# A transformer block on one core: normalised rows and k masks on VectorE, batched powers, paced v projections, blank matmuls in idle units

## The chip, the cores and the metric

The kernel runs on one core of a Trainium2 chip. The core has five engines that run side by side, each with its own queue of instructions taken in order: TensorE (PE in the profile; its weight loads are PEld) for matmuls, ScalarE (ACT) for table functions such as exp, VectorE (DVE) and GpSimd (POOL) for elementwise work, and SyncE (SP), which here issues all DMAs. Engines wait for each other through semaphores. Matmul results go to PSUM, eight banks of 128 x 512 fp32, which POOL does not read in this kernel; everything else lies in SBUF. The metric is the device time of one execution, in microseconds (us).

## What is computed

A layer norm, then attention and a gated feed-forward layer on the same normalised rows, both added to the input. In short:

```
xn  = (x - mean) / sqrt(var + 1e-5)                  # x: 2048 x 512, bf16
qkv = xn @ wqkv                                      # 32 heads of 16
p   = softmax(q @ k.T / 4)                           # per head, 2048 x 2048
att = (p @ v, heads side by side) @ wo
h   = max(xn @ W_gate, 0) * (xn @ W_up)              # 2048 x 1792
out = x + att + h @ W_down
```

The softmax is 32 x 2048 x 2048 exponentials. The kernel leaves out the subtraction of the maximum, and takes the sums from a column of ones beside v.

## The kernel before

The sequence is cut into 16 tiles of 128 rows (m or kt) and four blocks of 512 (b for keys, c4 for queries). The heads are cut into four groups gg of eight; in a group, ee picks the even or the odd heads and j one of four row strips of 32 partitions. kT holds each k projection twice, once with the odd and once with the even heads set to zero (the mask hmask), so that a score matmul can work on a strip of 32 rows.

The attention runs through tiles (c4, gg, ee, kt, j) in that order; three tiles make a **unit**, and there are 683 units. A unit is: up to three score matmuls into one of two score slots of three PSUM banks (L760), one exponential over 128 x 1536 from there into a slot of a ring of 13 (L772), and, as soon as all four strips of a kt are there, four matmuls of p with v (L736) into PSUM bank 0 of ps_b. Scores of unit u need the exponential of unit u-2 to be done, for the slot. When a (c4, gg, ee) is complete, `normalise` copies the sums out (L707), inverts them by way of two small DMAs, and POOL multiplies (L722).

Everything else is put between the units. `ln_block` makes the normalised and transposed rows xnT of a block: statistics on VectorE (L450, L451), variance plus eps and a power of -1/2 on POOL (L452, L454), the normalised row on POOL (L461), four transposes on TensorE (L478) and an eviction (L484 on ScalarE for block 0, L492 on VectorE for the others). x_sb has room for two blocks, so the loads of blocks 2 and 3 (L407) wait until the rows of blocks 0 and 1 are normalised. `proj_q`, `proj_k` and `proj_v` are chains of four matmuls (`mm_chain`, L510), nearly all into bank 1 of ps_b, with an eviction each; `proj_k` copies the bank to kp on VectorE (L539), and POOL makes the two masked halves from it (L542). Only the very first k projection is masked from PSUM by VectorE (L535). `glu` makes the hidden layer (L608, L612) and `out_rows` the output rows.

The order of each engine's queue is worked out on the host by a planner (`Graph.run`): every operation has an assumed duration and latency, a priority (lower goes first), and perhaps a unit `after` which it comes; the planner plays the program through by these numbers, and what it starts first on an engine stands first in that engine's queue. On the chip the order is fixed, and only the waits are real. The assumed durations are the second arguments of `G.op`: 450 ns for a normalised row and for a k mask on POOL, for example. Jobs (projections, hidden layer, output rows) are assigned to units in a list `plan`, at most one job step to a unit; a step is two matmuls of a chain. By the calls of `job` the steps are 24 for k, 30 for q, 224 for the hidden layer and 176 for output rows. The first group's k and all v projections stand outside this plan, with negative priorities.

At the start TensorE runs 14 matmuls on zeros (L567), and the first score may start when block 0 is normalised and its q and k are projected.

## Time and profile before

| | us |
|---|---|
| three runs of before | 1002.39, 1002.51, 1010.9; median 1002.51 |
| profiled execution, its own time | 1008.92 |
| its span, first to last instruction | 1007.0 |
| ScalarE busy in it | 929.3 |
| TensorE busy | 779.0 |
| VectorE busy | 173.1 |
| POOL busy | 138.5 |
| mean granted clock of TensorE | 0.848 |

The profile is one execution on the chip. Its page gives busy times, 40 slices of the span (the row PEclk is the clock granted to TensorE in tenths), the chain of work that ended last, and groups of instructions; the trace behind it answers for any stretch. A group row reads: line, engine, operation, what it writes and reads, shapes, count, then busy us and mean ns of one, then the idle time of the engine before them and what ended it. A timeline row reads: start and length in us, engine, line, operation, tiles, shapes, and how many instructions in a row it merges, with the idle time before the first in square brackets. A row of windows gives a stretch, its length, and for each engine the busy time and the count. Ends of matmuls are modelled, so a busy TensorE need not be one at its peak.

### The profile page before, as it was taken

How to read it: one execution, taken by the hardware profiler on the slowest of the kernel's cores; microseconds unless marked ns; L12 is line 12 of the kernel's file. 1: busy time of each engine (PE TensorE's matmuls, PEld its weight loads, DVE VectorE, ACT ScalarE, POOL GpSimd, SP SyncE). 2: the span in 40 equal slices, each digit the busy share in tenths (PEclk: the TensorE clock that was granted, in tenths of full speed). 3: DMA queues.
4: the chain of work that ended last, by engine and by line, in shares of the span. 5: the costliest groups of instructions: out<-in, count | busy, mean ns of one | idle time of the engine just before them, and what ended most of it. 6: DMA issues, size and time to landing. Idle time of an engine off the chain costs nothing.

```text
span 1007.0 us, 11864 instructions
## 1 busy us (share of the span) xinstructions
PE 779.0 (77%) x5078; PEld 184.7 (18%) x5166; DVE 173.1 (17%) x292; ACT 929.3 (92%) x690; POOL 138.5 (14%) x120
## 2 busy tenths in 40 slices
PE   4659877787778878877778888777777888888882
PEld 2212111111112211111111221111111221222220
DVE  3423212121100111211100002111110002321021
ACT  2449999999999999999999999999999999999992
POOL 8861504122000000000000000000000000000000
PEclk7679889887859987898867998888785999999995
DMA  4300200111000011111000012101100012221000
GB/s 125 116 1 25 62 17 17 32 32 33 12 22 22 18 37 43 43 43 35 10 11 27 27 38 48 38 16 33 43 12 22 26 34 54 53 54 27 22 12 33
DMA packets 84084, 34.59 MB, mean 34 GB/s; under 512 B 69952, under 2 KB 79936, under 8 KB 84032
## 3 DMA queue, kind: packets, MB, share of 16 engines
q1 hardware_dynamic: 84032, 33.83, 12.8%
q8 instruction: 41, 0.67, 0.3%
q14 instruction: 11, 0.09, 0.0%
HBM read 31.20 MB, written 2.36 MB: 33 GB/s over the span
## 4 chain that ended last, share of the span: by engine, by line
ACT 78%; PE 14%; POOL 5%; issue 1%; another core or an unknown queue 1%; DVE 1%; DMA 0%; ACTq 0%; SPq 0%
ACT ring L772 78%; PE ps_b L510 6%; PE ps_sc L760 5%; POOL xn_sb L461 3%; PE ps_b L736 3%; POOL rstd L454 1%; POOL kT L542 1%; POOL vare L452 0%; DMA x_sb<-in_A_x_dram 0%; DVE xn_sb L648 0%; DMA rsum<-o_sb 0%; DVE kp L539 0%; PE ps_sc L510 0%; PE ps_b L478 0%
## 5 line engine op out<-in xcount | busy, mean ns | idle before, releaser
L772 ACT ACTIVATE ring<-ps_sc 128x1536 bf16<-128x1536 f32 (+1 forms) x683 | 925.0, 1647 | 43.8 <-PE ps_sc L760 41.6
L760 PE MATMUL ps_sc<-qT,kT 32*128 32x512 bf16 x2048 | 300.9, 435 | 171.0 <-ACT ring L772 138.8
L736 PE MATMUL ps_b<-ring,v_aug 128*17 128x512 bf16 x2048 | 224.7, 432 | 5.0 <-DVE o_sb L707 2.0
L760 PEld LDWEIGHTS ps_sc<-qT,kT 32*128 32x128 bf16 x2048 | 67.6, 93 | 440.3 <-ACT ring L772 376.3
L722 POOL TENSOR_TENSOR x_sb<-o_sb,rb 128x512 bf16<-128x512 f32 x20 | 25.4, 1269 | 556.6 <-DMA rb<-rec_scr 556.6
L736 PEld LDWEIGHTS ps_b<-ring,v_aug 128*17 128x17 bf16 x2048 | 49.4, 88 | 198.8 <-issue 188.0
L510 PE MATMUL ps_b<-xnT,wus 128*128 128x512 bf16 x194 | 76.1, 469 | 5.4 <-issue 5.2
L608 DVE COPY up_sb<-ps_b 128x512 f32<-128x512 f32 x56 | 38.7, 692 | 239.7 <-PE ps_b L510 229.4
L510 PE MATMUL ps_b<-xnT,wgs 128*128 128x512 bf16 x213 | 70.8, 413 | 2.1 <-issue 1.8
L510 PE MATMUL ps_b<-Wd,hT 128*128 128x512 bf16 x206 | 66.5, 399 | 3.1 <-issue 3.1
L612 DVE SCALAR_TENSOR_TENSOR hT<-ps_b,up_sb 128x512 bf16<-128x512 f32 x56 | 38.7, 692 | 110.3 <-PE ps_b L510 107.8
L542 POOL TENSOR_SCALAR kT<-kp,hmask 128x512 bf16<-128x512 bf16 x30 | 46.6, 1566 | 65.6 <-DVE kp L539 64.1
L722 POOL TENSOR_TENSOR oT<-o_sb,rb 128x512 bf16<-128x512 f32 x12 | 15.2, 1270 | 233.5 <-DMA rb<-rec_scr 233.5
L707 DVE COPY o_sb<-ps_b 128x512 f32<-128x512 f32 x32 | 22.1, 690 | 133.4 <-PE ps_b L736 133.4
L648 DVE TENSOR_TENSOR xn_sb<-ps_b,xr_sb 128x512 bf16<-128x512 f32 x12 | 8.3, 692 | 146.8 <-PE ps_b L510 146.8
L461 POOL TENSOR_SCALAR xn_sb<-x_sb,mv,rstd 128x512 bf16<-128x512 bf16 x16 | 33.4, 2091 | 0.2
L510 PE MATMUL ps_b<-Wo_p,x_sb 128*128 128x512 bf16 x71 | 22.6, 387 | 11.8 <-POOL x_sb L722 10.9
L510 PE MATMUL ps_b<-xnT,Wk 128*128 128x512 bf16 x60 | 21.1, 444 | 1.1 <-issue 0.8
L510 PE MATMUL ps_b<-Wv,xnT 128*128 128x512 bf16 x60 | 20.7, 449 | 1.2 <-issue 0.4
L510 PEld LDWEIGHTS ps_b<-xnT,wus 128*128 128x128 bf16 x224 | 13.7, 103 | 34.0 <-issue 31.7
L510 PEld LDWEIGHTS ps_b<-xnT,wgs 128*128 128x128 bf16 x224 | 13.1, 99 | 31.3 <-issue 23.0
L510 PE MATMUL ps_b<-xnT,Wq 128*128 128x512 bf16 x52 | 17.5, 407 | 1.3 <-issue 1.3
(51 smaller groups left out, 161.8 us busy)
## 6 DMA issues: line engine op xcount, KB each, us to landing
rb<-rec_scr SPq DMA_DIRECT2D x32, 256.0 KB
wus<-in_B_W_up_dram SPq DMA_DIRECT2D x56, 128.0 KB, 2.5
wgs<-in_B_W_gate_dram SPq DMA_DIRECT2D x56, 128.0 KB, 2.3
xr_sb<-in_A_x_dram SPq DMA_DIRECT2D x16, 128.0 KB, 4.6
out_dram<-xn_sb SPq DMA_DIRECT2D x16, 128.0 KB, 1.7
Wd<-in_B_W_down_dram SPq DMA_DIRECT2D x1, 1792.0 KB, 8.0
x_sb<-in_A_x_dram SPq DMA_DIRECT2D x3, 512.0 KB, 4.0
Wv<-in_A_wqkv_dram SPq DMA_DIRECT2D x1, 512.0 KB, 7.8
```

Of the source, the lines that this page charges most:

```text
L454: G.op("POOL", 300, lambda e, m=m: e.tensor_tensor(rstd[:, m:m + 1], vare[:, m:m + 1], expo[:, 0:1], ALU.pow), reads=[t_ve, t_expo], write ...
L461: G.op("POOL", 450, lambda e, m=m, t=t_n: e.tensor_scalar(xn_sb[:, t.slot, :], xs(m), mv[:, m, 0:1], rstd[:, m:m + 1], op0=ALU.subtract, o ...
L510: ins = e.matmul(bank_of(tile, sub), l(), r(), start=(i == 0), stop=(i == n - 1))
L542: G.op("POOL", 450, lambda e, ee=ee: e.tensor_scalar(dsts[ee], kp[:, tkp.slot, :], hmask[:, ee:ee + 1], None, op0=ALU.mult), reads=[tkp, t ...
L608: G.op("DVE", 690, lambda e: e.tensor_copy(up_sb[:, tup.slot, :], bank_of(tu)), reads=[tu], writes=[tup], prio=slots[1])
L612: G.op("DVE", 690, lambda e: e.scalar_tensor_tensor(out=hT[:, FT * th.slot + ft, :], in0=bank_of(tg), scalar=0.0, in1=up_sb[:, tup.slot, : ...
L648: G.op("DVE", 690, lambda e: e.tensor_tensor(xn_sb[:, to_.slot, :], bank_of(t, sub), xr_sb[:, txr.slot, :] if first else resid(i), ALU.add ...
L707: G.op("DVE", 690, lambda e: e.tensor_copy(o_sb[:, to.slot, :], ps_b[:, 0, :]), reads=[tp], writes=[to], prio=-950, name="oev%d" % n)
L722: G.op("POOL", 1200, lambda e: e.tensor_tensor(oT_of(tn), o_sb[:, to.slot, :], rb[:, trb.slot, :], ALU.mult), reads=[to, trb], writes=[tn] ...
L736: ins = e.matmul(ps_b[32 * j:32 * j + VN, 0, :], v_aug[:, kt, 8 * gg + 2 * j + ee, 0:VN], ring[:, UNIT * tr.slot + i, :], start=(kt == 0), ...
L760: ins = e.matmul(ps_sc[:, 3 * ts.slot + i, :], kT[32 * j:32 * j + 32, 2 * gg + ee, 128 * kt:128 * kt + 128], qT[32 * j:32 * j + 32, t_q[(c ...
L772: return e.activation(ring[:, UNIT * tr.slot:UNIT * tr.slot + n, :], ps_sc[:, 3 * ts.slot:3 * ts.slot + n, :], ACTF.Exp, scale=0.25)
```

## The change

Six edits. (1) The normalised row (16 times) moves from POOL to VectorE, with 360 ns assumed. (2) For blocks 1 to 3 the variance and the power are done once for four tiles, [128, 4], after all four aggregates; block 0 keeps one per tile. (3) All k projections are masked by VectorE from PSUM, as the first one was; the buffer kp, its pool and its copy go, and the two masks follow each other. (4) The v projection of tile kt is held back in the plan until unit 1.3 kt, and keeps its negative priority then. (5) The memset of the ones beside v is no longer held until unit 2. (6) A unit beyond 24 to which no job step is assigned issues two matmuls of zeros by zeros into the first bank of its score slot, ahead of its score matmuls, which overwrite that bank; the planner's duration for the scores stays 330 ns. With the edits the planner works out new orders for all engines.

```diff
@@ -340,7 +340,6 @@
         hT = sb("hT", [128, NHT * FT, 512], BF16)
         up_sb = sb("up_sb", [128, NUP, 512], FP32)
         o_sb = sb("o_sb", [128, 2, 512], FP32)
-        kp = sb("kp", [128, 3, 512], BF16)
         rb = sb("rb", [128, 2, 512], FP32)
         rsum = sb("rsum", [128, 2, 16], FP32)
         rrec = sb("rrec", [128, 2, 16], FP32)
@@ -363,7 +362,6 @@
         P_oT = Pool("oT", 14)
         P_x = Pool("x", 2)
         P_xr = Pool("xr", 2)
-        P_kp = Pool("kp", 3)
 
 
         t_id, t_pid, t_mask, t_mask0, t_expo, t_warm, t_zero = (Tile() for _ in range(7))
@@ -384,7 +382,7 @@
                                                     base=0, pattern=[[-1, 128]], channel_multiplier=1),
              reads=[t_id], writes=[t_id], prio=-898)
         t_vones, t_woz = Tile(), Tile()
-        G.op("POOL", 2500, lambda e: e.memset(v_aug[:, :, :, DH:VN], 1.0), writes=[t_vones], prio=-500, after=2)
+        G.op("POOL", 2500, lambda e: e.memset(v_aug[:, :, :, DH:VN], 1.0), writes=[t_vones], prio=-500)
         G.op("POOL", 4200, lambda e: e.memset(Wo_p[:], 0.0), writes=[t_woz], prio=20, after=30)
 
         t_pvz = Tile("pvz", P_b, [0])
@@ -444,21 +442,31 @@
 
             first = b == 0
             t_rs = [Tile() for _ in range(4)]
+            t_mvs = Tile()
+
+            def inv(m, n, rd, wr):
+                t_ve = Tile()
+                G.op("POOL", 230, lambda e: e.tensor_scalar(vare[:, m:m + n], mv[:, m:m + n, 1], EPS, None, op0=ALU.add),
+                     reads=[rd], writes=[t_ve], prio=pr)
+                G.op("POOL", 400 + 160 * n, lambda e: e.tensor_tensor(rstd[:, m:m + n], vare[:, m:m + n], expo[:, 0:n], ALU.pow),
+                     reads=[t_ve, t_expo], writes=[wr], prio=pr)
             for i in range(4):
                 m = 4 * b + i
-                t_st, t_mv, t_ve = Tile(), Tile(), Tile()
+                t_st, t_mv = Tile(), Tile()
                 G.op("DVE", 640, lambda e, m=m: e.bn_stats(stats[:, m, :], xs(m)), reads=[t_xm[m]], writes=[t_st], prio=pr)
-                G.op("DVE", 120, lambda e, m=m: e.bn_aggr(mv[:, m, :], stats[:, m, :]), reads=[t_st], writes=[t_mv], prio=pr - 0.1)
-                G.op("POOL", 100, lambda e, m=m: e.tensor_scalar(vare[:, m:m + 1], mv[:, m, 1:2], EPS, None, op0=ALU.add),
-                     reads=[t_mv], writes=[t_ve], prio=pr)
-                G.op("POOL", 300, lambda e, m=m: e.tensor_tensor(rstd[:, m:m + 1], vare[:, m:m + 1], expo[:, 0:1], ALU.pow),
-                     reads=[t_ve, t_expo], writes=[t_rs[i]], prio=pr)
+                G.op("DVE", 130, lambda e, m=m: e.bn_aggr(mv[:, m, :], stats[:, m, :]), reads=[t_st], writes=[t_mv], prio=pr - 0.1)
+                t_mvs.w.append(G.ops[-1])
+                if first:
+                    inv(m, 1, t_mv, t_rs[i])
+            if not first:
+                inv(4 * b, 4, t_mvs, t_rs[0])
+                t_rs = [t_rs[0]] * 4
             if first:
                 tp0, tp1 = Tile("tp0", P_sc, [0]), Tile("tp1", P_sc, [1])
             for i in range(4):
                 m = 4 * b + i
                 t_n = Tile("xn", P_xn)
-                G.op("POOL", 450, lambda e, m=m, t=t_n: e.tensor_scalar(
+                G.op("DVE", 360, lambda e, m=m, t=t_n: e.tensor_scalar(
                     xn_sb[:, t.slot, :], xs(m), mv[:, m, 0:1], rstd[:, m:m + 1], op0=ALU.subtract, op1=ALU.mult),
                     reads=[t_xm[m], t_rs[i]], writes=[t_n], prio=pr + 0.2)
                 t_x[b].r.append(G.ops[-1])
@@ -510,7 +518,7 @@
                         ins = e.matmul(bank_of(tile, sub), l(), r(), start=(i == 0), stop=(i == n - 1))
                     return ins
                 G.op("PE", dur * (min(a + per, n) - a) + 100, fn, reads=reads, writes=[tile],
-                     prio=slots[k] if slots else prio, after=slots[k] if slots else None)
+                     prio=prio if prio < 0 else slots[k] if slots else prio, after=slots[k] if slots else None)
 
         def proj_q(c4, gg, prio=0.0, tile=None, sub=0, eng="DVE", slots=None):
             t = tile or Tile("pq", P_b, [1])
@@ -523,29 +531,21 @@
             else:
                 G.op("DVE", 690, lambda e: e.tensor_copy(qT[:, tq.slot, :], bank_of(t, sub)), reads=[t], writes=[tq], prio=prio)
 
-        def proj_k(gg, b, prio=0.0, tile=None, sub=0, slots=None, gap=0.5):
+        def proj_k(gg, b, prio=0.0, tile=None, sub=0, slots=None, gap=0.02):
             t = tile or Tile("pk", P_b, [0, 1] if (gg, b) in ((0, 1), (0, 2)) else [1])
             prio = slots[-1] if slots else prio
             mm_chain(t, [((lambda dt=dt: Wk[:, dt, 128 * gg:128 * gg + 128]), (lambda dt=dt: xnT[:, dt, 512 * b:512 * b + 512]))
                          for dt in range(DT)], [t_wk[gg], t_xnT[b]], prio, sub=sub, slots=slots)
             dsts = [kT[:, 2 * gg + ee, 512 * b:512 * b + 512] for ee in range(2)]
-            if (gg, b) == (0, 0):
-                for ee in range(2):
-                    tk = t_k[(gg, ee, b)] = Tile("k")
-                    G.op("DVE", 690, lambda e, ee=ee: e.tensor_scalar(dsts[ee], bank_of(t, sub), hmask[:, ee:ee + 1], None, op0=ALU.mult),
-                         reads=[t, t_masks[ee]], writes=[tk], prio=prio + 0.01 * ee)
-                return
-            tkp = Tile("kp", P_kp)
-            G.op("DVE", 690, lambda e: e.tensor_copy(kp[:, tkp.slot, :], bank_of(t, sub)), reads=[t], writes=[tkp], prio=prio)
             for ee in range(2):
                 tk = t_k[(gg, ee, b)] = Tile("k")
-                G.op("POOL", 450, lambda e, ee=ee: e.tensor_scalar(dsts[ee], kp[:, tkp.slot, :], hmask[:, ee:ee + 1], None, op0=ALU.mult),
-                     reads=[tkp, t_masks[ee]], writes=[tk], prio=prio + gap * ee)
+                G.op("DVE", 690, lambda e, ee=ee: e.tensor_scalar(dsts[ee], bank_of(t, sub), hmask[:, ee:ee + 1], None, op0=ALU.mult),
+                     reads=[t, t_masks[ee]], writes=[tk], prio=prio + gap * ee)
 
         def proj_v(kt, prio, allowed=(1,)):
             t = Tile("pv", P_b, list(allowed))
             mm_chain(t, [((lambda dt=dt: xnT[:, dt, 128 * kt:128 * kt + 128]), (lambda dt=dt: Wv[:, dt, :]))
-                         for dt in range(DT)], [t_wv, t_xnT[kt // 4]], prio)
+                         for dt in range(DT)], [t_wv, t_xnT[kt // 4]], prio, slots=[1.3 * kt] * 2)
             tv = t_v[kt] = Tile("v")
             G.op("DVE", 690, lambda e: e.tensor_copy(v_aug[:, kt, :, 0:DH], bank_of(t).rearrange("p (h d) -> p h d", h=H)),
                  reads=[t], writes=[tv], prio=prio)
@@ -571,10 +571,10 @@
         pb = Tile("pro", P_sc, [1])
         proj_q(0, 0, -790, tile=pb, sub=1, eng="ACT")
         tk_t = Tile("prok", P_b, [1])
-        proj_k(0, 0, -789, tile=tk_t, gap=8)
+        proj_k(0, 0, -789, tile=tk_t, gap=0.02)
         for b in range(1, NB):
             ln_block(b, -700 + 10 * b)
-            proj_k(0, b, -695 + 10 * b, gap=8)
+            proj_k(0, b, -695 + 10 * b, gap=0.02)
         for kt in range(NT):
             proj_v(kt, -684 + 10 * (kt // 4) + 0.1 * kt, allowed=(0, 1) if kt < 8 else (1,))
 
@@ -695,6 +695,7 @@
                 cur += 1.0
             plan.append((s[0] - lead, s, fn))
         plan.sort(key=lambda j: j[0])
+        busy = {int(p) for _, s, _ in plan for p in s}
 
 
         pv_tile, last_rec, where = {}, {}, {}
@@ -754,8 +755,12 @@
             ts = Tile("s%d" % u, P_sc)
             n = len(cl)
 
-            def sc(e, ts=ts, cl=cl):
+            def sc(e, ts=ts, cl=cl, idle=u > 24 and u not in busy):
                 ins = None
+                if idle:
+
+                    for _ in range(2):
+                        e.matmul(ps_sc[:, 3 * ts.slot, :], zeros[:, 0:128], zeros[:], start=True, stop=True)
                 for i, (c4, gg, ee, kt, j) in enumerate(cl):
                     ins = e.matmul(ps_sc[:, 3 * ts.slot + i, :], kT[32 * j:32 * j + 32, 2 * gg + ee, 128 * kt:128 * kt + 128],
                                    qT[32 * j:32 * j + 32, t_q[(c4, gg)].slot, :], start=True, stop=True, tile_position=(32 * j, 0))
```

## The prediction

> **What bounds the kernel now.** I read the page first: busy times, the granted clock over the span, and the chain that ended last.
>
> ```profile
> PE 779.0 (77%) x5078; PEld 184.7 (18%) x5166; DVE 173.1 (17%) x292; ACT 929.3 (92%) x690; POOL 138.5 (14%) x120
> PEclk7679889887859987898867998888785999999995
> ACT 78%; PE 14%; POOL 5%; issue 1%; another core or an unknown queue 1%; DVE 1%; DMA 0%; ACTq 0%; SPq 0%
> ```
>
> ScalarE, with its exponentials, is the limit; the rest of the chain is what keeps it from running. So the second view is ScalarE's timeline, whose rows end where it sat idle, and the third the same work in two windows.
>
> ```profile
> 16.68 1.08 ACT L484 ACTIVATE xnT<-ps_sc 128x512 bf16<-128x512 bf16 x2 [4.99 <-PE ps_sc L478]
> 22.80 2.79 ACT L772 ACTIVATE ring<-ps_sc 128x1536 bf16<-128x1536 f32 x2 [2.45 <-PE ps_sc L760]
> 44.59 1.45 ACT L772 ACTIVATE ring<-ps_sc 128x1536 bf16<-128x1536 f32 x1 [4.84 <-PE ps_sc L760]
> 60.90 2.79 ACT L772 ACTIVATE ring<-ps_sc 128x1536 bf16<-128x1536 f32 x2 [11.94 <-PE ps_sc L760]
> 76.29 46.24 ACT L772 ACTIVATE ring<-ps_sc 128x1536 bf16<-128x1536 f32 x34 [0.20 <-PE ps_sc L760]
> 777.11 211.97 ACT L772 ACTIVATE ring<-ps_sc 128x1536 bf16<-128x1536 f32 x158 [0.50 <-PE ps_sc L760]
> ```
>
> ```profile
> 22.80:76.29 53.49, 26.80 (x20) 0.72 0.19 55
> 76.29:989.10 912.81, 898.16 (x664) 0.87 0.12 30
> ```
>
> The last timeline row gives the undisturbed period: 158 exponentials in 211.97 us, 1.341 each. Against it the profiled execution splits into 22.8 before the first exponential; 53.5 in which 19 finish (25.5 at the period, 28.0 lost); 912.8 for the other 664 (890.4, 22.4 lost); and a tail of 17.9 from 989.1 to 1007.0. The change can win from the first 22.8, from the 28.0 and from the 22.4.
>
> **Front end.** Who kept ScalarE waiting there is read from the groups of instructions and POOL's timeline.
>
> ```profile
> L542 POOL TENSOR_SCALAR kT<-kp,hmask 128x512 bf16<-128x512 bf16 x30 | 46.6, 1566 | 65.6 <-DVE kp L539 64.1 <-DVE mv L451 1.5
> L461 POOL TENSOR_SCALAR xn_sb<-x_sb,mv,rstd 128x512 bf16<-128x512 bf16 x16 | 33.4, 2091 | 0.2
> L454 POOL TENSOR_TENSOR rstd<-vare,expo 128x1 f32<-128x1 f32 x16 | 8.8, 562 | 0.2
> L492 DVE COPY xnT<-ps_b 128x1024 bf16<-128x1024 bf16 x6 | 4.1, 690 | 11.9 <-PE ps_b L478 11.9
> L535 DVE TENSOR_SCALAR kT<-ps_b,hmask 128x512 bf16<-128x512 f32 x2 | 1.4, 746 | 8.5 <-PE ps_b L510 8.5
> L377 DVE TENSOR_SCALAR hmask<-pid 128x1 f32<-128x1 int32 x1 | 0.2, 154 | 0.0
> ```
>
> ```profile
> 5.13 1.09 POOL L454 TENSOR_TENSOR rstd<-vare,expo 128x1 f32<-128x1 f32 x2
> 6.22 4.17 POOL L461 TENSOR_SCALAR xn_sb<-x_sb,mv,rstd 128x512 bf16<-128x512 bf16 x2
> 10.37 0.41 POOL L452 TENSOR_SCALAR vare<-mv 128x1 f32<-128x1 f32 x2
> 48.37 4.17 POOL L461 TENSOR_SCALAR xn_sb<-x_sb,mv,rstd 128x512 bf16<-128x512 bf16 x2
> 58.62 3.11 POOL L542 TENSOR_SCALAR kT<-kp,hmask 128x512 bf16<-128x512 bf16 x2
> ```
>
> POOL normalises a 128-row tile in 2.09 us and masks a k half in 1.57, with no idle time before the normalised rows. The 11.94 us hole ahead of the exponential at 60.90 is the two masks of row 58.62, queued behind normalised rows of the next block (48.37 on). The orders were planned with 450 ns for either.
>
> **Its pieces after the change.** The normalised row on VectorE is not in the trace. Ends: 0.15 us (a one-column tensor_scalar, L377) and 0.75 (L535, from PSUM). Nearest is L492, bf16 to bf16: (690-154)/1024 = 0.52 ns an element, so 154 + 512 x 0.52 = 0.42 us, which I take. A k mask costs the measured 0.70 (1.41 for two); the copy to kp (0.69) goes, so VectorE gains 0.7 per projection. The batched power over four columns lies between 0.56 (one) and 2.25 (four); I take 1.1.
>
> ```profile
> 5.99 0.30 DVE L451 BATCH_NORM_AGGREGATE mv<-stats 128x2 f32<-128x6 f32 x2
> 10.07 1.29 DVE L450 BATCH_NORM_STATS2 stats<-x_sb 128x6 f32<-128x512 bf16 x2 [3.78 <-DMA x_sb<-in_A_x_dram]
> 17.82 1.89 PE L510 MATMUL ps_sc<-xnT,Wq 128*128 128x512 bf16 x4 [0.75 <-ACT xnT L484]
> 16.01 11.55 SPq L407 DMA_DIRECT2D x_sb<-in_A_x_dram  x2
> ```
>
> First exponential: statistics end at 6.3 as before. POOL's first two powers end at 6.22, and the other two (0.41 + 1.09) now follow at once, by 7.7. The rows come from VectorE at about 6.7, 7.1, 7.9 and 8.4, the last transposes end near 8.9 and ScalarE's last eviction near 9.7 instead of 17.76. From Wq's first matmul (17.82) to the first exponential it is 4.98 us, unchanged: 9.7 + 5.0 = 14.7, so 8.1 us won. VectorE is then free of block 1's statistics (10.07 to 13), so the first masks lose little.
>
> After it every block of k lasts 16/3 units, 7.15 us of exponentials. A block asks of VectorE four statistics and aggregates (3.4), four rows (1.7), two transposed copies (1.4), two masks (1.4) and four v copies (2.8): 10.7 us. Three blocks behind 10.07 would end at 42, and the third must be masked by 14.7 + 16 x 1.341 = 36.2. But the second masks (2.1 in all) may come a pass later, and so, thanks to the new pacing and the 13 slots of the ring, may some eight v copies (5.5); with block 0's masks (1.4) VectorE needs until 10.07 + 32.1 - 7.6 + 1.4 = 36. It just fits if dense. TensorE is as full there: four v matmuls take 1.7 us at half clock (17.82: 1.89 for four, starts 0.42 apart). The x loads move too: SyncE issued blocks 2 and 3 at 16.01 and about 27.2, behind POOL's rows; now near 8.5 and 17, and the weight loads queued behind them come earlier with them. For order and waits I take 8 us lost in place of 28.0, with ends 0 (it fits) and 28 (VectorE as jammed as POOL). The memset of v_aug (2.29) drops into POOL's idle time ahead of its first variance at 4.76; cover gone, it costs at most 2.3. Later k masks hold bank 1 0.7 us longer, 12 times: between 0 and 8.4; I take 0, since VectorE is busy 17% and TensorE has slack between score groups, shown next.
>
> **The blank matmuls.** Windows of all engines at single-clock stretches; the columns are busy time of PE, PEld, DVE, ACT, POOL, then granted clock.
>
> ```profile
> 6.00:8.00 2.00, 0.45 (x3) 0.00 (x0) 0.29 (x3) 0.00 (x0) 2.00 (x2) 1.00 1.05 328
> 73.70:77.10 3.40, 3.40 (x15) 0.76 (x13) 0.69 (x1) 3.20 (x3) 2.75 (x1) 0.50 0.00 0
> 77.10:118.00 40.90, 36.33 (x264) 9.43 (x267) 13.46 (x21) 40.78 (x32) 13.65 (x9) 1.00 0.15 42
> 275.10:305.80 30.70, 24.64 (x137) 4.35 (x135) 0.94 (x2) 29.98 (x23) 1.27 (x1) 0.50 0.06 18
> 305.80:367.20 61.40, 51.12 (x358) 12.64 (x362) 5.35 (x9) 61.40 (x47) 2.54 (x2) 1.00 0.10 29
> ```
>
> From 275.1 to 305.8 no projection fills the units (scores and p times v alone): the clock stays at 0.50. From 305.8 to 367.2 nearly every unit has its two projection matmuls: 1.00 throughout, and no idle ScalarE. The 22.4 us are lost where such units alternate: projection matmuls then meet the half clock and delay the scores. Two blank matmuls make an idle unit as full as a busy one. Zeros count: the clock is 1.00 at 6 to 8, behind nothing but the zero-operand warm-up. By the list of jobs 24 + 30 + 224 + 176 = 454 of 683 units are busy; some 208 of those beyond unit 24 get blanks.
>
> ```profile
> 849.68 2.81 ACT L772 ACTIVATE ring<-ps_sc 128x1536 bf16<-128x1536 f32 x2
> 849.86 0.39 PE L760 MATMUL ps_sc<-qT,kT 32*128 32x512 bf16 x3
> 850.19 0.60 PE L510 MATMUL ps_b<-xnT,wgs 128*128 128x512 bf16 x2
> 850.72 0.39 PE L736 MATMUL ps_b<-ring,v_aug 128*17 128x512 bf16 x4
> ```
>
> ```profile
> 43.94 0.61 PE L760 MATMUL ps_sc<-qT,kT 32*128 32x512 bf16 x3
> 63.70 0.39 PE L760 MATMUL ps_sc<-qT,kT 32*128 32x512 bf16 x3
> 64.14 1.45 ACT L772 ACTIVATE ring<-ps_sc 128x1536 bf16<-128x1536 f32 x1 [0.44 <-PE ps_sc L760]
> ```
>
> The blanks stand in front of the scores and behind the wait for the score bank, so they lengthen ScalarE's loop. At full clock scores start 0.18 after an exponential (849.68 to 849.86), two full matmuls take 0.53 (850.19 to 850.72), and an exponential follows its scores by 0.44 (63.70 to 64.14): 1.15, under the period of 1.341. They cost nothing, with 0.19 to spare. At half clock the matmuls take about 0.95 (two at 0.42, and 0.1 for the switch) and the scores 0.65 (43.94 to 44.59): 1.78, or 0.44 late per idle unit. But then TensorE is busy without a break, and in row 73.70 such a stretch (3.40 of 3.40) is followed by 41 us at 1.00. I take the 22.4 as won whole, with ends 0 won and, below nothing, the loss of the rival below.
>
> **Sum.** 14.7 + 683 x 1.341 (915.9) + 8 + 0 + 17.9 = 956.5 us of span. The profiled execution of before took 1008.9 for a span of 1007.0; with the same 1.9 I predict **958 us**, 5.0% under its own time and 4.4% under the median of 1002.5. The profiled execution lies 6.4 above that median, and I subtract nothing for it: what spreads the runs is probably the clock, which is wanted steady here.
>
> **Rivals.** (a) *VectorE, or TensorE under it, jams the front end*: the block-by-block waits stay at some 23 us lost instead of 8, giving 973. For it: demand fits only if dense. Against: nothing there is as slow as POOL's 2.09. (b) *The blanks leave the clock as it is*, and the 22.4 stay: 981. Against: rows 275.10 and 305.80 differ by just such matmuls. In the Trainium skill, TensorE: Matmul & The Clock Gate, section HAM oscillation, the rule is "no PE-idle gaps >~3.4µs"; by that rule the small gaps of idle units would not lower the clock, filling them would not raise it, and the time would be the 981 of this rival. The trace disagrees: 0.50 in row 275.10 with TensorE busy 24.64 of 30.70 us. (c) *Blanks late at full clock too*, by 0.15 us a unit: 208 x 0.15 = 31, giving 989. Against: 0.19 to spare; for it: the loads of the blank weights may not hide as L510's do. (d) *Slower*: blanks keep the loop at half clock, 0.44 late in every idle unit, 208 x 0.44 = 92: 1050. It decides from (1002.5 - 958)/208 = 0.21 per unit, half of the idle units at half clock. Against: row 73.70.
>
> **Numbers.** Forecast 0.58, (a) 0.20, (b) 0.08, (c) 0.11, (d) 0.03. The forecast's own range is 948 to 968 (first exponential and front-end loss off by some 10). The whole range, 946 to 980, takes in (a) and leaves out (c), (d) and most of (b). A difference under about 1% this kernel's measurement cannot tell from none; 1% under the median is 992.5, so faster 0.95 (all but (d) and late versions of (c)), within 1% 0.03, slower 0.02.
>
> **What would show it.** First exponential near 14.7; the last hole over 2 us before about 45; no POOL row of xn_sb or kT; the row on VectorE near 0.42 us. Granted clock near 1.0 in nearly all slices between the front end and the tail, and ScalarE rows at 1.341 per exponential in stretches that had idle units. Wrong would be holes of ScalarE ended by PE in idle units, or slices at half clock; or a front end in which VectorE is busy nine tenths and ScalarE waits on it.

## The result and the profile after

The changed kernel takes 971.6 us, the median of three runs (968.6 to 971.9), against 1002.5 before: 0.965 of the time, 95% interval 0.958 to 0.972. The profiled execution took 971.9 us, its span is 970.0. 958 was predicted, with 946 to 980 as the whole range: the direction and that range held, the gain was 30.9 us where 44.5 was forecast. The time lies outside the 948 to 968 that the prediction named as the forecast's own range, in the part that was kept for a jammed front end.

From the page of the changed kernel, busy times, granted clock by slices, and the chain that ended last:

```profile
PE 804.9 (83%) x5482; PEld 205.6 (21%) x5584; DVE 192.6 (20%) x323; ACT 925.9 (95%) x690; POOL 54.0 (6%) x56
PEclk8899999999999999999999999999999999999996
ACT 82%; PE 12%; DVE 3%; DMA 1%; issue 1%; SPq 0%; POOLq 0%; ACTq 0%
```

The clock row is the first thing to compare: 25 of 40 slices stood below 9 tenths before, now only the two of the front end and the tail do. POOL had 5% of the chain and has none now but its queue. ScalarE's timeline after, to be read as before (start, length, the idle time ahead in brackets):

```profile
11.39 1.08 ACT L492 ACTIVATE xnT<-ps_sc 128x512 bf16<-128x512 bf16 x2 [2.29 <-PE ps_sc L486]
17.64 13.66 ACT L777 ACTIVATE ring<-ps_sc 128x1536 bf16<-128x1536 f32 x10 [2.59 <-PE ps_sc L765]
35.54 4.14 ACT L777 ACTIVATE ring<-ps_sc 128x1536 bf16<-128x1536 f32 x3 [4.24 <-PE ps_sc L765]
42.11 1.45 ACT L777 ACTIVATE ring<-ps_sc 128x1536 bf16<-128x1536 f32 x1 [2.43 <-PE ps_sc L765]
48.98 28.49 ACT L777 ACTIVATE ring<-ps_sc 128x1536 bf16<-128x1536 f32 x21 [1.87 <-PE ps_sc L765]
354.93 330.70 ACT L777 ACTIVATE ring<-ps_sc 128x1536 bf16<-128x1536 f32 x244 [0.29 <-PE ps_sc L765]
```

The hole of 11.94 us is gone. But the last row shows that something is left: 244 exponentials in 330.7 us are 1.355 each, with no hole that the row names, where before 158 in a row took 1.341 each.

To compare kernels I split the one trace of each in the same way: the start of the first exponential, the time lost from there to the start of the exponential 40 later (against 40 x 1.341), the time lost behind that (against 643 x 1.341), and the tail behind the last. These parts and 683 x 1.341 = 915.9 make up the span; the starts are read from the trace. The "front end" is the stretch until the k of all four blocks is there, and "front loss" is what ScalarE loses in it.

| kernel | median us | ratio to before, 95% interval | first exp | front loss | loss behind |
|---|---|---|---|---|---|
| before | 1002.5 | | 22.8 | 28.2 | 22.2 |
| changed | 971.6 | 0.965 (0.958 to 0.972) | 17.6 | 10.4 | 8.3 |
| predicted, by its profile terms | 958 | | 14.7 | 8 | 0 |
| no blanks | 984.2 | 0.978 (0.973 to 0.983) | 17.5 | 9.8 | 22.9 |
| blanks alone | 994.8 | 0.989 (0.984 to 0.994) | 22.2 | 30.0 | 5.9 |
| one blank | 978.9 | 0.973 (0.967 to 0.979) | 17.7 | 9.8 | 21.7 |
| blanks one unit later | 964.6 | 0.958 (0.954 to 0.962) | 18.5 | 9.3 | 1.5 |
| block 0's rows first | 967.6 | 0.962 (0.959 to 0.966) | 14.9 | 9.2 | 6.2 |
| memsets out of the way | 965.3 | 0.960 (0.956 to 0.964) | 17.6 | 5.5 | 6.2 |
| v unpaced | 971.2 | 0.965 (0.962 to 0.969) | 18.1 | 10.6 | 8.4 |
| v eight units later | 974.9 | 0.970 (0.967 to 0.973) | 17.6 | 16.5 | 7.0 |
| rows on POOL again | 984.3 | 0.977 (0.973 to 0.981) | 23.1 | 19.3 | 6.2 |
| masks on POOL again | 971.1 | 0.964 (0.960 to 0.967) | 18.0 | 10.9 | 8.0 |
| three mends together | 958.8 | 0.952 (0.948 to 0.955) | 16.0 | 6.4 | 1.5 |
| the same, v later | 967.3 | 0.960 (0.956 to 0.965) | 15.5 | 14.6 | 1.8 |

The kernel before was run again beside each group of four; its medians there were 1004.8, 1005.5 and 1008.5, so ratios compare better than microseconds. The medians are of three runs for before and changed and of four for the others, the parts of the one profiled execution. The tail is 17.5 to 18.1 in every trace.

### The profile page after: what moved, and what is told of

Read it like the earlier page. It is cut to its first block, busy times and chain, and to the rows that moved or that the text cites. A ratio compares the mean times of both kernels' runs of the same rounds, so it can differ in the third digit from the quotient of the medians.

```text
span 970.0 us, 12635 instructions
## 1 busy us (share of the span) xinstructions
PE 804.9 (83%) x5482; PEld 205.6 (21%) x5584; DVE 192.6 (20%) x323; ACT 925.9 (95%) x690; POOL 54.0 (6%) x56
## 3 DMA queue, kind: packets, MB, share of 16 engines
q1 hardware_dynamic: 84032, 33.83, 13.5%
## 4 chain that ended last, share of the span: by engine, by line
ACT 82%; PE 12%; DVE 3%; DMA 1%; issue 1%; SPq 0%; POOLq 0%; ACTq 0%
ACT ring L777 82%; PE ps_b L518 4%; PE ps_sc L763 3%; PE ps_sc L765 3%; PE ps_b L737 2%; DVE kT L542 1%; DMA x_sb<-in_A_x_dram 1%; DVE xn_sb L469 1%; DMA rb<-rec_scr 0%; PE ps_sc L518 0%; DVE v_aug L550 0%; DVE stats L456 0%; PE ps_b L486 0%; DVE xn_sb L648 0%; DMA rsum<-o_sb 0%
## 5 line engine op out<-in xcount | busy, mean ns | idle before, releaser
L765 PE MATMUL ps_sc<-qT,kT 32*128 32x512 bf16 x2048 | 268.0, 387 | 96.1 <-ACT ring L777 70.9
L737 PE MATMUL ps_b<-ring,v_aug 128*17 128x512 bf16 x2048 | 202.0, 388 | 2.9 <-DVE o_sb L708 1.8
L763 PE MATMUL ps_sc<-zeros 128*128 128x512 bf16 x398 | 122.1, 384 | 25.1 <-ACT ring L777 16.3
L765 PEld LDWEIGHTS ps_sc<-qT,kT 32*128 32x128 bf16 x2048 | 66.2, 91 | 351.9 <-ACT ring L777 253.7
L737 PEld LDWEIGHTS ps_b<-ring,v_aug 128*17 128x17 bf16 x2048 | 49.2, 88 | 169.4 <-issue 159.2
L518 PE MATMUL ps_b<-xnT,wgs 128*128 128x512 bf16 x211 | 65.3, 386 | 2.5 <-issue 2.0
L518 PE MATMUL ps_b<-xnT,wus 128*128 128x512 bf16 x198 | 62.4, 389 | 5.7 <-issue 3.8
L518 PE MATMUL ps_b<-Wd,hT 128*128 128x512 bf16 x206 | 63.7, 384 | 2.7 <-issue 2.5
L763 PEld LDWEIGHTS ps_sc<-zeros 128*128 128x128 bf16 x418 | 24.6, 97 | 88.4 <-ACT ring L777 79.8
L542 DVE TENSOR_SCALAR kT<-ps_b,hmask 128x512 bf16<-128x512 f32 x32 | 22.6, 746 | 26.6 <-PE ps_b L518 26.5
L518 PE MATMUL ps_b<-Wo_p,x_sb 128*128 128x512 bf16 x70 | 22.4, 387 | 1.1 <-issue 1.1
L518 PE MATMUL ps_b<-xnT,Wk 128*128 128x512 bf16 x60 | 18.9, 407 | 1.9 <-DVE kT L542 1.1
L518 PEld LDWEIGHTS ps_b<-xnT,wus 128*128 128x128 bf16 x224 | 13.0, 97 | 27.5 <-issue 23.1
L518 PE MATMUL ps_b<-Wv,xnT 128*128 128x512 bf16 x61 | 17.1, 388 | 1.7 <-DVE xnT L500 0.9
L518 PEld LDWEIGHTS ps_b<-xnT,wgs 128*128 128x128 bf16 x224 | 12.7, 97 | 26.7 <-issue 22.9
```

Of the source, the lines that this page charges most:

```text
L518: ins = e.matmul(bank_of(tile, sub), l(), r(), start=(i == 0), stop=(i == n - 1))
L542: G.op("DVE", 690, lambda e, ee=ee: e.tensor_scalar(dsts[ee], bank_of(t, sub), hmask[:, ee:ee + 1], None, op0=ALU.mult), reads=[t, t_masks ...
L737: ins = e.matmul(ps_b[32 * j:32 * j + VN, 0, :], v_aug[:, kt, 8 * gg + 2 * j + ee, 0:VN], ring[:, UNIT * tr.slot + i, :], start=(kt == 0), ...
L763: e.matmul(ps_sc[:, 3 * ts.slot, :], zeros[:, 0:128], zeros[:], start=True, stop=True)
L765: ins = e.matmul(ps_sc[:, 3 * ts.slot + i, :], kT[32 * j:32 * j + 32, 2 * gg + ee, 128 * kt:128 * kt + 128], qT[32 * j:32 * j + 32, t_q[(c ...
```

## The experiments

**What the blanks bring, and what the rest does.** The changed kernel without blanks, and the kernel before with nothing but blanks.

```diff
-                if idle:
-
-                    for _ in range(2):
-                        e.matmul(ps_sc[:, 3 * ts.slot, :], zeros[:, 0:128], zeros[:], start=True, stop=True)
```

> The changed kernel without its blank matmuls. Theory: the blanks hold the clock, and that is worth the part of the 22.4 us lost behind the front end that the changed kernel no longer loses (it loses 8.8): some 13.6 us, so about 985 us (980 to 991), half-clock stretches of 30 us back, a mean clock near 0.87, first exponential and front end as in the changed kernel. Rival: the front end brought the whole gain and the blanks give back what they win: 970 to 974.

> The kernel before with the blank matmuls alone. Theory: front end as before (first exponential near 22.8, steady from 76), clock near 1.0 behind it, 13.6 us less: about 989 us (985 to 994). Rival (blanks give back what they win): 1000 to 1003.

984.2 and 994.8 us. The clock row of the page without blanks shows the dips back; with blanks alone only the front end and the tail are below 9:

```profile
PEclk8899787897589988897759988888866998999995
```

```profile
PEclk7679999999999999999999999999999999999997
```

The two halves are separate: without blanks 22.9 us are lost behind the front end (22.2 before), with blanks alone 5.9, and the front ends are close to those of the kernels they come from. The ratios multiply, 0.978 x 0.989 = 0.967, close to 0.965 for both. The second kernel came out 0.8 us above what was expected of it.

**Why the blanks do not bring all 22.** TensorE's timeline of the changed kernel, where a hidden-layer job ends (L518 is a job's pair, L763 the blanks, L765 scores, L737 p times v):

```profile
384.30 0.61 PE L518 MATMUL ps_b<-xnT,wgs 128*128 128x512 bf16 x2
385.00 0.61 PE L763 MATMUL ps_sc<-zeros 128*128 128x512 bf16 x2
385.53 0.39 PE L765 MATMUL ps_sc<-qT,kT 32*128 32x512 bf16 x3
385.86 0.60 PE L518 MATMUL ps_b<-xnT,wgs 128*128 128x512 bf16 x2
386.39 0.39 PE L737 MATMUL ps_b<-ring,v_aug 128*17 128x512 bf16 x4
386.72 0.61 PE L763 MATMUL ps_sc<-zeros 128*128 128x512 bf16 x2
387.26 0.39 PE L765 MATMUL ps_sc<-qT,kT 32*128 32x512 bf16 x3
```

The unit that begins with the blanks at 385.00 also has the job's last pair at 385.86. From blanks to blanks it takes 1.72 us (0.53 + 0.33 + 0.53 + 0.33), more than the period of 1.341, and the next scores are late. Going through the trace unit by unit behind unit 50, every job step is found exactly one unit behind the one that the plan assigns to it, in all 432 cases: `after` holds a step behind the exponential of its unit, whose scores are by then in the queue. So behind unit 50, 48 units with blanks (of 209 in all) have a step as well, and 48 others have neither. Of 14.4 us lost behind unit 50 (against 1.331, the median period), 11.6 stand at the 48 doubled ones and the unit behind each. The experiment moves the blanks by that one unit:

```diff
-            def sc(e, ts=ts, cl=cl, idle=u > 24 and u not in busy):
+            def sc(e, ts=ts, cl=cl, idle=u > 24 and u - 1 not in busy):
```

> Blanks in unit u if unit u-1 has no job step assigned. In the trace of the changed kernel every job step runs one unit behind the one assigned to it, so 48 units have both blanks and a step and 48 have neither. Theory: these doubled units are what ScalarE still waits for (11.6 of the 14.4 us lost behind unit 50 at 1.331 us each); with the shift each unit has one or the other, and the time falls to about 960 us (957 to 964), with exponentials at 1.33 to 1.34 us throughout. Rival: blanks ahead of the scores delay them in every idle unit, or the short half-clock windows are what costs: 968 or more.

964.6 us, with 1.5 us lost behind the front end. The single row of ScalarE's timeline, and of the windows of that trace between front end and tail (columns as before, the clock behind POOL's), show it:

```profile
83.02 862.10 ACT L777 ACTIVATE ring<-ps_sc 128x1536 bf16<-128x1536 f32 x642 [0.18 <-PE ps_sc L765]
```

```profile
45.90:946.90 901.00, 767.99 (x5270) 191.28 (x5368) 154.42 (x244) 897.58 (x669) 39.34 (x31) 1.00 0.13 33
```

642 exponentials in 862.1 us are 1.343 each, at full clock for 901 us. The time lies just above the expected 957 to 964. The rival's first half falls: blanks ahead of the scores cost next to nothing where the unit has no step. Its second half holds for a part. The changed kernel's trace has three short windows at half clock behind its front end, of 3.4 us each (from 166.6, 350.9 and 682.0). The traces of three later runs, "block 0's rows first", "memsets out of the way" and "rows on POOL again", have the same blanks as the changed kernel and no such window there, and lose 6.2 instead of 8.3; three more, with one to four windows, lose 7.0 to 8.4. So of the 6.8 us that the shift brought in the traces, some 4.7 belong to the doubled units and some 2.1 to those windows. The units at which the 11.6 us stood still lose 4.5 in the shifted trace, so not all of that was the doubling's. Whether the units that had neither blanks nor a step brought the windows on was not tested.

The other way to make doubled units shorter is one blank in place of two.

```diff
-                    for _ in range(2):
+                    for _ in range(1):
```

> One blank matmul in place of two. Theory of the doubled units: each doubled unit is 0.22 us shorter, some 4 us of the 11.6 stay, and if one blank still holds the clock the time is about 964 us (961 to 967). Rival: one blank is too little for the clock, which falls in idle stretches as without blanks: 975 to 985 and mean clock under 0.93.

978.9 us (974.6 to 985.1, the profiled execution at the upper end): the rival's case. One blank does not hold the clock through. In a stretch without jobs it stays at half, with TensorE busy 29.2 of 30.7 us, while ScalarE does 22 exponentials, one per 1.4 us (windows of that trace):

```profile
248.80:279.50 30.70, 29.22 (x143) 5.69 (x145) 0.94 (x2) 29.22 (x22) 1.27 (x1) 0.50 0.06 18
```

**Why the first exponential comes at 17.6.** VectorE's timeline of the changed kernel:

```profile
6.47 0.71 DVE L469 TENSOR_SCALAR xn_sb<-x_sb,mv,rstd 128x512 bf16<-128x512 bf16 x2
7.81 0.41 DVE L469 TENSOR_SCALAR xn_sb<-x_sb,mv,rstd 128x512 bf16<-128x512 bf16 x1 [0.63 <-POOL rstd L451]
9.68 0.69 DVE L456 BATCH_NORM_STATS2 stats<-x_sb 128x6 f32<-128x512 bf16 x1 [1.46 <-DMA x_sb<-in_A_x_dram]
10.29 0.40 DVE L469 TENSOR_SCALAR xn_sb<-x_sb,mv,rstd 128x512 bf16<-128x512 bf16 x1
```

The fourth row of block 0, at 10.29, whose power was ready near 8.3, stands behind a statistic of block 1, which waits for its load until 9.68. The order is the planner's, which took the load to land earlier.

In the experiment rows0 holds block 0's four rows, and `order` puts them ahead.

```diff
                 G.op("DVE", 640, lambda e, m=m: e.bn_stats(stats[:, m, :], xs(m)), ..., prio=pr,
+                     order=rows0 if b == 1 else ())
```

> The changed kernel with one order added: VectorE takes block 0's four normalised rows ahead of block 1's statistics. In the changed kernel the fourth row, ready near 8.3 us, stands behind a statistic that waits for block 1's load until 9.66, and starts at 10.29. Theory: that place in VectorE's queue is what makes the first exponential come at 17.6 and not at the predicted 14.7; it comes at 15.3 (14.8 to 15.8), and the time falls by about 2 us to 969.5. Rival: the first exponential is held by something behind the row (the q and k projections, the loads of Wq and Wk) and stays above 17; or it comes early and the 2 us go into the later wait for block 2.

967.6 us, first exponential at 14.88, and the gain is not lost further on (front loss 9.2). The first theory holds. Of the 5.9 us by which this trace is shorter than the changed kernel's, 2.8 stand ahead of the first exponential and 2.1 behind the front end, where it has no window at half clock. VectorE's timeline of this run shows what now holds block 0's masks:

```profile
8.93 1.29 DVE L458 BATCH_NORM_STATS2 stats<-x_sb 128x6 f32<-128x512 bf16 x2 [0.20 <-DMA x_sb<-in_A_x_dram]
13.31 0.41 DVE L472 TENSOR_SCALAR xn_sb<-x_sb,mv,rstd 128x512 bf16<-128x512 bf16 x1 [1.49 <-POOL rstd L453]
13.64 1.40 DVE L549 TENSOR_SCALAR kT<-ps_b,hmask 128x512 bf16<-128x512 f32 x2
```

TensorE's k projection is done by 12.3, but the masks stand behind a row of block 1, which waits for its batched power.

**Why block 3 is late.** VectorE's and POOL's timelines of the changed kernel show two pairs that run side by side:

```profile
1.64 1.87 DVE L373 TENSOR_SCALAR pid<-pid 128x2 int32<-128x2 int32 x1
...
28.48 1.36 DVE L469 TENSOR_SCALAR xn_sb<-x_sb,mv,rstd 128x512 bf16<-128x512 bf16 x4
...
35.72 4.54 DVE L469 TENSOR_SCALAR xn_sb<-x_sb,mv,rstd 128x512 bf16<-128x512 bf16 x4
```

```profile
1.09 2.29 POOL L385 MEMSET v_aug<- 128x512 bf16 x1
...
35.63 3.51 POOL L386 MEMSET Wo_p<- 128x4096 bf16 x1
```

Four rows take 1.36 us alone and 4.54 beside the memset of Wo_p: the first of them takes 3.57 us, the others 0.40 each behind it. A two-column operation (0.16 us before) takes 1.87 beside the memset of v_aug. POOL now reaches both memsets early, since its rows are gone. The experiment makes one wait for the masks hmask, the other for block 3's rows (rows3):

```diff
-        G.op("POOL", 2500, lambda e: e.memset(v_aug[:, :, :, DH:VN], 1.0), writes=[t_vones], prio=-500)
+        G.op("POOL", 2500, lambda e: e.memset(v_aug[:, :, :, DH:VN], 1.0), reads=[t_mask0], writes=[t_vones], prio=-500)
...
+        for o in rows3:
+            t_woz.w[0].deps[o] = True
```

> The changed kernel with POOL's two long memsets out of VectorE's way: the one of v_aug waits for the masks, the one of Wo_p for block 3's normalised rows. In the changed kernel a VectorE operation that takes 0.16 us took 1.87 beside the first memset, and block 3's four rows took 4.54 us beside the second, where block 2's took 1.36. Theory: the memset on POOL blocks the normalised row on VectorE; the four rows fall to 1.4 us, the waits ahead of the exponentials at 42.1 and 49.0 shrink by 3 us in all, and the time falls to about 968.5 us. Rival: the rows are slow for another reason (their loads, the power before them) and stay at 4.5, time 971 to 972.

965.3 us, front loss 5.5. VectorE's timeline of this kernel, the same two operations:

```profile
1.64 0.16 DVE L373 TENSOR_SCALAR pid<-pid 128x2 int32<-128x2 int32 x1
...
35.70 1.38 DVE L471 TENSOR_SCALAR xn_sb<-x_sb,mv,rstd 128x512 bf16<-128x512 bf16 x4
```

Both are back at their own length. The waits of 2.43, 0.59 and 1.87 us ahead of block 3's exponentials shrink to one of 0.34, so the gain in the front end is that of the memset of Wo_p. The first exponential stays at 17.6: moving the memset of v_aug won nothing there. The wait of 4.24 us for block 2 stays, at 4.25. The Trainium skill, SBUF — State Buffer, section SBUF: two separate sides, says that VectorE in its two-port modes and POOL share a pair of ports as an exclusive lock, held for the whole instruction. The trace agrees: a held VectorE operation ends only after the memset, and has its usual length once that is moved. In which mode VectorE worked the profile does not show.

**Is VectorE the bound between?** It is busy 13.30 of 13.70 us ahead of the hole of 4.24:

```profile
17.60:31.30 13.70, 11.61 (x81) 4.49 (x81) 13.30 (x31) 13.64 (x10) 1.28 (x2) 1.00 0.29 78
```

I took the v copies to be what could be moved out.

```diff
-                         for dt in range(DT)], [t_wv, t_xnT[kt // 4]], prio, slots=[1.3 * kt] * 2)
+                         for dt in range(DT)], [t_wv, t_xnT[kt // 4]], prio, slots=[1.3 * kt + 8] * 2)
```

> The changed kernel with each v projection eight units later (from unit 1.3 kt + 8). In the changed kernel VectorE is busy 13.3 of the 13.7 us from 17.6 to 31.3, and ScalarE waits 4.24 us for block 2's k masks. Theory: VectorE is the bound of that stretch and the v copies in it, which the ring would let come later, are what stands ahead of block 2; the wait of 4.24 falls under 1.5 and the time by 3 to 5 us, to 967 to 969. Rival: block 2 is late by its own chain (load, statistics, power, transposes) and the wait stays above 3; or the v copies come back as a wait further on, time 971 or more.

> The changed kernel without the pacing of the v projections, as they were before. Theory (VectorE is the bound of the front end): v copies crowd in ahead of the later blocks, and the front end loses 14 to 18 us in place of 10; time 975 to 980. Rival: the planner puts them late anyway, and nothing changes: 970 to 973.

Neither theory held. Without the pacing (the diff's `slots` left out) nothing changes: 971.2. With v eight units later the time grows to 974.9, the front loss to 16.5, and the wait for block 2 to 6.71. TensorE's timeline there:

```profile
30.30 3.14 PE L518 MATMUL ps_b<-Wv,xnT 128*128 128x512 bf16 x12
35.84 1.04 PE L518 MATMUL ps_b<-xnT,Wk 128*128 128x512 bf16 x4 [2.39 <-DVE v_aug L550]
```

Three v chains now stand in TensorE's queue ahead of block 2's k projection, and it waits for their evictions. The memset of Wo_p still falls on block 3's rows, which now stand ahead of block 2's masks; the later run with that out of the way (below) settles that it is not the memset alone. So the question stays open: VectorE is full ahead of that hole, but the late v changed TensorE's order as well, and no other run settles what holds block 2.

**What moving rows and masks was worth each.** One of the two goes back to POOL with its old assumed 450 ns, the other stays.

```diff
-                G.op("DVE", 360, lambda e, m=m, t=t_n: e.tensor_scalar(
+                G.op("POOL", 450, lambda e, m=m, t=t_n: e.tensor_scalar(
```

> The changed kernel with the normalised rows back on POOL (450 ns assumed, as before), masks and the rest as changed. Theory: the rows are the main part of the front end's gain. At 2.09 us a row POOL needs 8.4 + 1.3 us a block, more than the 7.15 that a block lasts, and block 0's four in a line; first exponential 20 to 23, front-end loss 15 to 20, time 982 to 988. Rival: the masks behind the rows were the loss before, and rows alone on POOL cost little: 971 to 976.

For the masks, the copy to kp, its pool and the two POOL operations of the kernel before are put back:

```diff
-                G.op("DVE", 690, lambda e, ee=ee: e.tensor_scalar(dsts[ee], bank_of(t, sub), hmask[:, ee:ee + 1], None, op0=ALU.mult),
-                     reads=[t, t_masks[ee]], writes=[tk], prio=prio + gap * ee)
+                G.op("POOL", 450, lambda e, ee=ee: e.tensor_scalar(dsts[ee], kp[:, tkp.slot, :], hmask[:, ee:ee + 1], None, op0=ALU.mult),
+                     reads=[tkp, t_masks[ee]], writes=[tk], prio=prio + gap * ee)
```

> The changed kernel with the k masks back on POOL (copy to kp on VectorE, 450 ns assumed), rows on VectorE. Theory: with the rows gone POOL has room for two masks of 1.57 us a block, and VectorE, full in the front end, loses 0.7 a block; each block's k comes some 1.6 later, but only what is not hidden counts: 969 to 975. Rival: the masks on POOL are as costly as the rows (a queue, and POOL reads holding up VectorE's rows): 978 or more.

Rows on POOL: 984.3 us, 12.6 more than the changed kernel, first exponential at 23.1. POOL's and ScalarE's timelines there:

```profile
17.79 8.26 POOL L469 TENSOR_SCALAR xn_sb<-x_sb,mv,rstd 128x512 bf16<-128x512 bf16 x4
```

```profile
50.61 4.32 ACT L777 ACTIVATE ring<-ps_sc 128x1536 bf16<-128x1536 f32 x3 [9.92 <-PE ps_sc L765]
```

Masks on POOL: 971.1 us, the same as the changed kernel. That does not say that the move of the masks brought nothing. POOL's and ScalarE's timelines there:

```profile
37.18 3.12 POOL L552 TENSOR_SCALAR kT<-kp,hmask 128x512 bf16<-128x512 bf16 x2 [3.30 <-DVE kp L549]
...
50.44 3.51 POOL L388 MEMSET Wo_p<- 128x4096 bf16 x1
```

```profile
39.61 8.16 ACT L787 ACTIVATE ring<-ps_sc 128x1536 bf16<-128x1536 f32 x6 [6.35 <-PE ps_sc L775]
```

The memset of Wo_p runs here only at 50.44, behind the masks of block 3 and so behind its rows. The run to compare with is therefore the one with the memsets out of the way and the masks on VectorE. It loses 5.5 us in the front end, and this one 10.9: the wait for block 2 is 6.35 in place of 4.25, and block 1 and block 3 wait 1.65 and 1.68. By this comparison masks on POOL cost some 5 us, which the memset, no longer in the way, hides. The batched power was not taken back alone, so what it brought is not known.

**Together.** The blanks one unit later, block 0's rows first, and the memsets moved; then the same with v eight units later.

> The changed kernel with the three mends that helped alone: blanks shifted by one unit, block 0's rows ahead of block 1's statistics, memsets out of VectorE's way. Theory (three separate losses that add): first exponential 14.9, front end 5 lost, 1.5 lost behind it, tail 17.8: 14.9 + 915.9 + 5 + 1.5 + 17.8 = 955 of span and 957 us. Rival (the front end's mends overlap, or one loss turns up further on): 960 or more.

> As the run with all three mends, and v projections eight units later. With the late v alone block 2 waited 6.71 us, but there the memset of Wo_p had moved onto block 3's rows, and a chain of 12 v matmuls stood in TensorE's queue ahead of block 2's k. Theory: without the memset in the way the late v frees VectorE and the wait for block 2 falls under 2.5: 952 to 955 us. Rival: the order of TensorE's queue is what holds block 2 (v chains ahead of its k projection), and the wait stays at 4 or more: 957 to 962.

958.8 us (958.0 to 959.9), 0.952 of before, the fastest of all. It lies between the theory's 957 and the rival's 960. In the traces the three mends alone took 6.8 us behind the front end, 2.8 off the first exponential and 4.9 off the front loss, 14.5 in all; together they shorten the span by 12.6. The first exponential came at 16.0, not 14.9. VectorE's timeline, with TensorE's k projection done by 11.9:

```profile
10.04 1.29 DVE L458 BATCH_NORM_STATS2 stats<-x_sb 128x6 f32<-128x512 bf16 x2 [1.76 <-DMA x_sb<-in_A_x_dram]
14.42 0.41 DVE L472 TENSOR_SCALAR xn_sb<-x_sb,mv,rstd 128x512 bf16<-128x512 bf16 x1 [1.49 <-POOL rstd L453]
14.75 1.40 DVE L549 TENSOR_SCALAR kT<-ps_b,hmask 128x512 bf16<-128x512 f32 x2
```

Block 0's masks stand behind a row of block 1 that waits for the batched power, as in the run with block 0's rows first. What is later here by 1.1 us is the first statistic of block 1, which waits for its load until 10.04 (8.93 there); why the load came later is not known. The wait for block 2 is 4.10 us in this trace, the largest left in the front end. VectorE is busy 13.58 of the 14.6 us before it.

With v later it is 967.3 us, slower than theory (952 to 955) and rival (957 to 962). ScalarE's timeline:

```profile
34.21 8.16 ACT L786 ACTIVATE ring<-ps_sc 128x1536 bf16<-128x1536 f32 x6 [4.59 <-PE ps_sc L774]
47.43 5.48 ACT L786 ACTIVATE ring<-ps_sc 128x1536 bf16<-128x1536 f32 x4 [5.05 <-PE ps_sc L774]
```

Block 2 waits 4.59 with no memset beside it, as the rival said: again three v chains stand ahead of its k projection in TensorE's queue. But it waits 4.10 without the late v too, so the order is not shown to be the whole of it. The longest wait there is now one of 5.05 us for block 3.

## Why the prediction was right, and where it was not

The profiled span is 13.5 us over the predicted 956.5. By its terms: 2.9 in the first exponential, 2.4 in the front loss, 8.3 behind it, and 0.1 less in the tail.

*First exponential, 14.7 predicted, 17.6 measured.* The durations were right: the row takes 0.41 us (0.42 taken), the chain from Wq to the first exponential was left nearly as long. The step that failed is "The rows come from VectorE at about 6.7, 7.1, 7.9 and 8.4": it put the rows on an engine and left out what that engine's own queue would have in front of them. The run with that one order mended gave 14.88. That this is so near 14.7 is in part luck: the four matmuls of Wq took 1.04 us there and not the 1.89 of the sum, and the masks then waited behind a row of block 1, which the sum did not have either.

*Front end, 8 lost predicted, 10.4 measured.* The batched power was right (1.04 us for four columns, 1.1 taken), and VectorE was as full as the sum had it (13.30 of 13.70 us). What the sum did not have is the memset of Wo_p on block 3's rows: with both memsets moved the 10.4 fall to 5.5, less than the 8 forecast. Most of what is left is the wait of 4.2 us for block 2, whose cause stays open. The memset of v_aug was priced by POOL's idle time alone; what it delayed was VectorE, by 1.7 us in one operation, with nothing lost at the first exponential. The pacing of v, taken as what keeps v copies out of the way, does nothing here.

*The masks.* Their cost was right (0.75 mean, two in 1.41), and the longer hold of bank 1 cost nothing that shows: the run with the masks back on POOL loses 8.0 behind the front end, against 8.3. But the reading of the hole of 11.94 as "the two masks of row 58.62, queued behind normalised rows of the next block" should have gone a step further: most of the queue was the rows, which alone on POOL bring a hole of 9.92 back. The masks alone on POOL bring one of 6.35 where there is one of 4.25 without them.

*Blanks, 22.4 won predicted, 13.9 measured* (22.2 lost before, 8.3 after). The mechanism held: the clock is at 1.00 behind the front end but for three windows of 3.4 us, and without blanks the dips are back. The count was right (418 weight loads of zeros, 209 units). The step that failed is "Two blank matmuls make an idle unit as full as a busy one": the list of jobs was read as the order of the queue, and the queue runs one unit behind the list. The loop of 1.15 us stood for units with blanks alone, and these keep the period; 48 units behind unit 50 had blanks and a step, and the one shown above took 1.72. With the blanks shifted, 1.5 us are lost and the predicted zero is nearly there.

*Rivals.* (a), a jammed front end, was half there: an order and a memset are shown to be 2.8 and 4.9 us of it, and the sign that the prediction gave for it, VectorE busy nine tenths ahead of a wait, stands before block 2. Whether VectorE's load causes that wait is not shown. (b), a clock that does not follow, is refuted by the pair of runs with and without blanks. The rule cited there from the Trainium skill (TensorE: Matmul & The Clock Gate, section HAM oscillation), by which idle gaps of over some 3.4 us lower the clock, does not cover the run with one blank either: 0.50 with TensorE busy 29.2 of 30.7 us. (c), blanks late at full clock in every idle unit, is refuted by the shifted blanks, with 1.5 us lost. (d) did not come. But the reason given against it, that TensorE busy without a break brings the clock up (row 73.70), is too weak: with one blank TensorE was busy nearly without a break and stayed at 0.50. The largest piece of the front end's gain is the rows' move: first exponential and front loss together fell by 23.0 us, and 14.4 of these are lost again with the rows on POOL. This and the sum's form (first exponential, period, losses, tail) came out as argued.

## What to carry to other kernels

When an operation moves to another engine, look at two things besides its duration: what stands ahead of it in the new engine's queue, and which operations of the other engine, freed to run earlier, now run beside it. When filler work is put where a plan says an engine is idle, check in a trace that the work really runs where the plan puts it; here one unit's offset cost a third of what the filler could bring (6.8 of 20.7 us, some 2.1 of them by way of short half-clock windows). And fill that is to keep a clock up has to be enough of it: here two blanks a unit did, and one left the clock low in the long idle stretches. An amount between was not tried. When a part of a change is taken back and the time stays, look in the trace whether another loss moved at the same time, as the memset did with the masks. When one mend brings a forecast time back, look in its trace whether the terms of the sum came back too; here two of them were off in opposite ways.

## What the runs showed of the hardware that I had not expected

A memset on POOL, which has no input, holds up VectorE's row for its whole length: one row takes 3.57 us beside a memset of 3.51, and about 0.40 otherwise. In a stretch without jobs one full matmul of 512 columns per unit (1.4 us), beside scores and p times v, leaves the clock at 0.50 while TensorE counts as 95% busy (29.22 of 30.70); with two in each unit without a step it is 1.00 for 901 us, with TensorE 85% busy (767.99). So the busy share in the profile does not tell which clock is granted. Part of that share is the low clock itself: three scores take 0.61 us at half clock and 0.39 at full. Where the threshold lies was not measured.
